# Two weight loads are moved behind later writes of x: the second expert tile's w1, and the quarters' first weights

## The chip, the cores and the metric

The kernel runs on one core of a Trainium2 chip. The metric is the device time of one execution in microseconds (us). A change under 0.3% (1.3 us) can hardly be told from no change here.

## The reference

Three layers run one after the other on 2 x 768 tokens of 512 numbers, in float32: decaying linear attention (8 heads), a feed-forward layer with a convolution along the sequence and a gate, and a mixture of 8 experts. Of the last two:

```
h = np.maximum(x @ w_in, 0.0)
...
return (h * gate @ w_out).astype(np.float32)
...
            h = np.maximum(x[b, s] @ w1[e], 0.0)
            out[b, s] = p[e] * (h @ w2[e])
```

The expert `e` of a token is the argmax of its eight logits, or the expert of the token before it where a local gate says so. So the tokens of one expert are known only when the second layer's output x is known.

## The kernel before

The second layer ends in `ffn_out`, which makes x in twelve tiles of 128 tokens: six of sequence 0 and six of sequence 1. Each tile is accumulated on TensorE (PE) into `x_ps` (lines 133 to 135), copied to SBUF by ScalarE (ACT, line 486), and written to the DRAM tensor `xs` by a DMA that SyncE (SP) issues (line 488). The copy of the last two tiles stays in SBUF as `xl`.

Around these tiles VectorE (DVE) makes the tables of the routing: `ei` (which expert each tile of the last layer uses) and `it` (which tokens it takes).

The last layer works in expert tiles of 128 tokens of one expert: 11 whole tiles, and two groups of four quarters of 32 tokens, each quarter with an expert of its own. A tile's tokens are brought from `xs` by an indirect DMA that GpSimd (POOL) issues (`gather`, line 724, into `xg`). The first two tiles, j = 0 and 1, gather from the first ten tiles of x alone; what they need of the last two comes on PE from `xl` by one-hot matrices (line 816). Every other gather reads all twelve tiles, the first of them that of the quarters' group 0 (`gather(NTILE)`), then that of tile 2.

Weights come over SP's queue, 512 KB for each DMA. `fetch(j, 0)` brings w1 of tile j in four DMAs into `r` (line 695), `fetch(j, 1)` w2; for j > 1 they are skipped when tile j - 2 had the same expert. `fetch_q(g, which, i)` brings an eighth of the weights of a group of quarters, one DMA for each of the four experts, into the buffers `qc` and `qs1l` in turn (line 705). A quarter's matmuls are `hq_ps` (line 889) and `yq_ps` (line 911).

The order of SP's queue is the order of the code. In the loop over `units` one pass adds two of the eight k-blocks to one tile of x, so passes 8, 12, 16 and 20 end tiles nine to twelve of x (t = 2 to 5 of sequence 1). Behind the loop `experts` begins with `fetch(1, 1)` and `fetch_q(0, 0, 1)`. Of SP's DMAs each waits until the one eight places ahead of it has landed (its lane, `DMAHW0` to `DMAHW7`), beside what its buffer needs.

Of the kernel before, what the change touches and what calls it, by code (L numbers as in the profile page):

```python
# [91 lines left out]
def tile_kernel(ctx, tc, cat, cst, qT, kT, kN, vN, w_in, conv_w, w_out, wg, w1, w2, out):  # L92
# [378 lines left out]
    def ffn_out(b, t, ms):  # L471

        ts = slice(t * P, (t + 1) * P)
        if ms[0] == 0:
            OUT[b, t] = psb.tile([P, DM], F32, tag="x2", name="x2_ps")
        ps = OUT[b, t]
        for m in ms:
            g = hg[b, m]
            mm3(ps, g[:, 0, ts], g[:, 1, ts], wo_hi[:, m, :], wo_lo[:, m, :], m == 0, m == 7)
        if ms[-1] == 7:  # L480
            if b == B - 1 and t >= NG - 2:
                xn = xpool[0].tile([P, DM], F32, name=f"xl{t}", bufs=1)
                LAST.append(xn)
            else:
                xn = rt.tile([P, DM], F32, name="xn", bufs=2)
            se.activation(out=xn, in_=OUT.pop((b, t)), func=AF.Copy)  # L486
            r = b * S + t * P
            sy.dma_start(out=xs[r:r + P, :], in_=xn)
# [183 lines left out]
    def home(tag):  # L672
        return big if tag[0] == "s" else ws if tag == "c4" else wx

    def expert_at(n):
        return sy.value_load(ei[0:1, 0, n:n + 1], min_val=0, max_val=E - 1)
# [6 lines left out]
    def fetch(j, which):  # L683

        src = (w1, w2)[which].rearrange("e p a n -> e p (a n)")
        kw = {}
        if j == 0:
            src = src[0]
        else:
            src = src[bass.ds(expert_at(j), 1)].rearrange("o p n -> (o p) n")  # L690
            if j > 1:
                kw = dict(cond=sy.value_load(ei[0:1, 1, j:j + 1], min_val=0, max_val=1), cond_hint=True)
        dst = raw(j % 2, which)
        for i in range(4):
            sy.dma_start(out=dst[:, i, :], in_=src[:, i * 1024:(i + 1) * 1024], **kw)

    def fetch_q(g, which, i):

        tag = QSLOT[nq[0] % 2]
        nq[0] += 1  # L700
        QW[g, which, i] = w = home(tag).tile([P, 4, 1024], F32, tag=tag, name="q" + tag)
        src = (w1, w2)[which].rearrange("e p a n -> e p (a n)")
        for u in range(4):
            one_e = src[bass.ds(expert_at(NTILE + 4 * g + u), 1)].rearrange("o p n -> (o p) n")
            sy.dma_start(out=w[:, u, :], in_=one_e[:, i * 1024:(i + 1) * 1024])

    def cut(j, which, i):

        tag = SLOT[ncut[0] % len(SLOT)]
        ncut[0] += 1  # L710
        w = home(tag).tile([P, 2, 2, 1024], F32R, tag=tag, name="w" + tag)
        for h in range(2):
            r = RAW[j % 2, which][:, 2 * i + h, :]
            se.activation(out=w[:, 0, h, :], in_=r, func=AF.Copy)  # L714
            ve.tensor_tensor(out=w[:, 1, h, :], in0=r, in1=w[:, 0, h, :].bitcast(F32), op=ALU.subtract)  # L715
        W[j, which, i] = w.rearrange("p s h n -> p s (h n)")
# [3 lines left out]
    def gather(j, n=NT):  # L720

        X[j] = xg = xpool[0].tile([P, DM], F32, name="xg")
        po.memset(xg, 0.0)
        return po.indirect_dma_start(out=xg, out_offset=None, in_=xs[0:n], in_offset=bass.IndirectOffsetOnAxis(ap=it[:, j:j + 1], axis=0),  # L724
                                     bounds_check=n - 1, oob_is_err=False)
# [43 lines left out]
    for n, (t, ms) in enumerate(units, 1):  # L769
        ffn_out(1, t, ms)  # L770
        for step in STEPS.get(n, ()):
            next(step, done)
        if n == 8:
            fetch(1, 0)
        if n in (10, 14):
            cut(0, 0, n // 14)
        if n == 13:
            fetch_q(0, 0, 0)
            for j in range(2):
                gather(j, NT - 2 * P)  # L780
    p2_stack.close()
    q_stack.close()
    lg_stack.close()
# [276 lines left out]
```

## Time and profile before

| | |
|---|---|
| time, median of 3 runs | 433.12 us (432.42 to 433.65) |
| profiled execution: its time, its span | 433.53 us, 431.8 us |
| PE busy | 406.7 us (94%) |
| DVE, ACT, POOL busy | 290.1, 259.4, 91.6 us |
| bytes by DMA, mean rate | 86.59 MB, 201 GB/s |
| granted TensorE clock, mean | 0.993 |

The span runs from the first to the last instruction of the one profiled execution; its time is 1.7 us longer. PE is busy nearly throughout, so the places where it is not are what a change of order can touch. The DMA engines carry 201 GB/s as a mean, but not evenly.

### The profile page before, as it was taken

The page shows a single profiled execution, that of the slowest core. Times are in us where ns is not written, and L with a number is a line of the kernel's source. Part 1 is how long each engine was busy: PE and PEld are TensorE (multiplying, and loading weights), DVE is VectorE, ACT ScalarE, POOL GpSimd, SP SyncE. Part 2 cuts the span into 40 slices and gives each one's busy share as a digit, 9 for nine tenths or more (in the row PEclk, how much of TensorE's full clock was granted, in tenths as well). Part 3 has the DMA queues.
Part 4 walks back from the last instruction along what each step waited for, and adds up shares of the span by engine and source line. Part 5 has one row for each costly group of instructions (what it writes and reads, how often), then busy time and mean ns, then how long its engine had stood idle before and what let it go on. Part 6 is the DMA issues. An engine that isn't in the chain of part 4 may idle for free.

```text
span 431.8 us, 7294 instructions
## 1 busy us (share of the span) xinstructions
PE 406.7 (94%) x2412; PEld 327.2 (76%) x2412; DVE 290.1 (67%) x518; ACT 259.4 (60%) x429; POOL 91.6 (21%) x92
## 2 busy tenths in 40 slices
PE   8898999997999999999999899999989999999991
PEld 7787897896898778989768676867738676776881
DVE  3798789798766350477899057968663796858650
ACT  2787677666755212566604166869555786958560
POOL 5256664213000000000000330205212132111210
PEclk9999999999999999999999999999999999999997
DMA  7989773320000101000296999999979999675001
GB/s 239 380 289 399 257 218 87 96 92 1 2 2 0 49 29 46 26 0 2 82 355 214 358 382 350 347 385 407 379 272 330 393 367 362 266 257 205 34 26 37
DMA packets 27324, 86.59 MB, mean 201 GB/s; under 512 B 3598, under 2 KB 4622, under 8 KB 27280
## 3 DMA queue, kind: packets, MB, share of 16 engines
q1 hardware_dynamic: 25200, 79.76, 50.6%
q0 software_dynamic: 2080, 6.29, 3.8%
q8 instruction: 21, 0.34, 0.3%
q14 instruction: 23, 0.19, 0.1%
HBM read 105.18 MB, written 6.55 MB: 259 GB/s over the span
## 4 chain that ended last, share of the span: by engine, by line
PE 35%; issue 26%; DMA 18%; DVE 14%; ACT 3%; POOL 2%; SPq 0%; POOLq 0%; DVEq 0%
DMA out_dram<-yo,it 15%; PE h_ps L133 5%; PE h_ps L135 4%; PE h_ps L134 4%; PE x_ps L133 4%; PE x_ps L134 3%; PE x_ps L135 3%; PE y L297 3%; PE s_ps L279 3%; DVE cc L350 2%; DMA kv<-in_kN_dram 2%; DVE na L149 2%; PE inc L287 2%; DVE na L150 1%; PE y L299 1%
## 5 line engine op out<-in xcount | busy, mean ns | idle before, releaser
L133 PE MATMUL h_ps<-xT,wih 128*128 128x384 f32 x128 | 46.5, 363 | 2.3 <-ACT wc L192 2.3
L350 DVE SCALAR_TENSOR_TENSOR cc<-h,cw,cc 128x768 f32<-128x768 f32 x32 | 35.1, 1097 | 16.8 <-ACT cc L347 16.8
L860 POOL DMA_INDIRECT out_dram<-yo,it x13 | 16.7, 1283 | 137.1 <-ACT yo L859 137.1
L724 POOL DMA_INDIRECT xg<-xs,it x13 | 18.8, 1442 | 125.5 <-DMA qc<-in_w_dram 118.6
L134 PE MATMUL h_ps<-xT,wih 128*128 128x384 f32 x128 | 43.1, 337 | 0.0
L135 PE MATMUL h_ps<-xT,wil 128*128 128x384 f32 x128 | 43.1, 336 | 0.0
L133 PE MATMUL x_ps<-woh,hg 128*128 128x512 f32 x96 | 38.5, 401 | 0.0
L134 PE MATMUL x_ps<-wol,hg 128*128 128x512 f32 x96 | 37.5, 391 | 0.0
L135 PE MATMUL x_ps<-woh,hg 128*128 128x512 f32 x96 | 37.5, 390 | 0.0
L715 DVE TENSOR_TENSOR ws0l<-r,ws0l 128x1024 fp32r<-128x1024 f32 x22 | 26.0, 1222 | 16.3 <-ACT ws0l L714 16.1
L297 PE MATMUL y<-at,vz 128*128 128x128 f32 x192 | 30.6, 281 | 1.7 <-DMA kv<-in_kN_dram 0.9
L715 DVE TENSOR_TENSOR ws0h<-r,ws0h 128x1024 fp32r<-128x1024 f32 x22 | 26.0, 1222 | 8.3 <-ACT ws0h L714 8.2
L715 DVE TENSOR_TENSOR wc<-r,wc 128x1024 fp32r<-128x1024 f32 x22 | 25.9, 1221 | 7.9 <-ACT wc L714 7.9
L714 ACT ACTIVATE ws0l<-r 128x1024 fp32r<-128x1024 f32 x22 | 22.1, 1052 | 13.6 <-PE y L135 13.6
L153 POOL TENSOR_TENSOR na<-na,raw 128x512 int32<-128x512 int32 (+1 forms) x17 | 21.9, 1290 | 38.2 <-DVE na L150 12.6
L715 DVE TENSOR_TENSOR ws1h<-r,ws1h 128x1024 fp32r<-128x1024 f32 x22 | 26.0, 1222 | 6.0 <-ACT ws1h L714 4.0
L279 PE MATMUL s_ps<-qz,kq 128*128 128x256 f32 x96 | 29.0, 384 | 1.0 <-DVE qz L248 1.0
L714 ACT ACTIVATE wc<-r 128x1024 fp32r<-128x1024 f32 x22 | 22.1, 1054 | 11.3 <-PE g L135 11.3
L297 PEld LDWEIGHTS y<-at,vz 128*128 128x128 f32 x192 | 25.3, 191 | 4.3 <-DVE xT L302 2.3
L133 PEld LDWEIGHTS h_ps<-xT,wih 128*128 128x128 f32 x128 | 24.1, 188 | 5.5 <-ACT wc L192 2.6
L281 DVE TENSOR_TENSOR at<-s_ps,ca 128x256 f32<-128x256 f32 x48 | 20.2, 420 | 11.6 <-PE s_ps L279 11.5
L486 ACT ACTIVATE xn<-x_ps 128x512 f32<-128x512 f32 x10 | 6.0, 599 | 32.8 <-PE x_ps L135 15.5
(231 smaller groups left out, 1041.5 us busy)
## 6 DMA issues: line engine op xcount, KB each, us to landing
r<-in_w_dram SPq DMA_DIRECT2D x88, 512.0 KB
qc<-in_w_dram SPq DMA_DIRECT2D x32, 512.0 KB
qs1l<-in_w_dram SPq DMA_DIRECT2D x32, 512.0 KB
raw<-in_w_in_dram SPq DMA_DIRECT2D x8, 512.0 KB
raw<-in_w_out_dram SPq DMA_DIRECT2D x8, 512.0 KB
kq<-in_qT_dram SPq DMA_DIRECT2D x7, 384.0 KB
kq<-in_kT_dram SPq DMA_DIRECT2D x7, 384.0 KB
kv<-in_vN_dram SPq DMA_DIRECT2D x7, 384.0 KB
```

The costliest lines, as they stand in the source:

```text
L133: te.matmul(ps, lhi, rhi, start=first, stop=False)
L134: te.matmul(ps, lhi, rlo, start=False, stop=False)
L135: te.matmul(ps, llo, rhi, start=False, stop=last)
L153: po.tensor_tensor(out=a, in0=a, in1=lo, op=ALU.add)
L279: te.matmul(ps, self.kq[:, 0, tok], self.qz[:, :, tok], start=True, stop=True)
L281: ve.tensor_tensor(out=self.at[c], in0=ps, in1=self.dm, op=ALU.mult)
L297: te.matmul(y, vz[:, c, j, :], at[:, j, :], start=(j == 0), stop=(c == 0 and j == 1))
L350: ve.scalar_tensor_tensor(out=cc, in0=h[:, i:i + S], scalar=cw[:, m, i:i + 1], in1=cc, op0=ALU.mult, op1=ALU.add)
L714: se.activation(out=w[:, 0, h, :], in_=r, func=AF.Copy)
L715: ve.tensor_tensor(out=w[:, 1, h, :], in0=r, in1=w[:, 0, h, :].bitcast(F32), op=ALU.subtract)
L724: return po.indirect_dma_start(out=xg, out_offset=None, in_=xs[0:n], in_offset=bass.IndirectOffsetOnAxis(ap=it[:, j:j + 1], axis=0), bound ...
L860: po.indirect_dma_start(out=out, out_offset=bass.IndirectOffsetOnAxis(ap=it[:, j:j + 1], axis=0), in_=yo, in_offset=None, bounds_check=NT ...
```

## The change

`fetch(1, 0)` moves from pass 8 (behind the write of tile nine of x) to pass 12 (behind that of tile ten). `fetch_q(0, 0, 0)` moves from pass 13 to pass 16 (behind the write of tile eleven). Nothing is added or removed.

```
         ffn_out(1, t, ms)
         for step in STEPS.get(n, ()):
             next(step, done)
-        if n == 8:
+        if n == 12:
             fetch(1, 0)
         if n in (10, 14):
             cut(0, 0, n // 14)
         if n == 13:
-            fetch_q(0, 0, 0)
             for j in range(2):
                 gather(j, NT - 2 * P)
+        if n == 16:
+            fetch_q(0, 0, 0)
```

SP's queue around the last four writes of x, before (`r_2127` is the buffer of `fetch(1, 0)`, `qc_2404` that of `fetch_q(0, 0, 0)`, `xn` and `xl` are tiles of x; of four like DMAs the first and the last stand here):

```order
L488 DMA xs<-xn 128x512 [waits DMAHW3_49,Activation_49]
L676 TENSOR_LOAD ei [waits DVE_49]
L695 DMA r_2127<-in_w_dram 128x1024 [waits DMAHW4_49]
...
L695 DMA r_2127<-in_w_dram 128x1024 [waits DMAHW7_49]
L488 DMA xs<-xn 128x512 [waits DMAHW0_49,Activation_49]
L705 DMA qc_2404<-in_w_dram 128x1024 [waits DMAHW1_49]
...
L705 DMA qc_2404<-in_w_dram 128x1024 [waits DMAHW4_49]
L488 DMA xs<-xl_2478 128x512 [waits DMAHW5_49,Activation_49]
L488 DMA xs<-xl_2506 128x512 [waits DMAHW6_49,Activation_49]
```

And the same place after the change (`qc_2440` is the buffer of `fetch_q(0, 0, 0)` there):

```order
L488 DMA xs<-xn 128x512 [waits DMAHW3_49,Activation_49]
L488 DMA xs<-xn 128x512 [waits DMAHW4_49,Activation_49]
L676 TENSOR_LOAD ei [waits DVE_49]
L695 DMA r_2127<-in_w_dram 128x1024 [waits DMAHW5_49]
...
L695 DMA r_2127<-in_w_dram 128x1024 [waits DMAHW0_49]
L488 DMA xs<-xl_2437 128x512 [waits DMAHW1_49,Activation_49]
L705 DMA qc_2440<-in_w_dram 128x1024 [waits DMAHW2_49]
...
L705 DMA qc_2440<-in_w_dram 128x1024 [waits DMAHW5_49]
L488 DMA xs<-xl_2506 128x512 [waits DMAHW6_49,Activation_49]
```

The write of tile ten now stands ahead of the four `r` loads, and the write of tile eleven ahead of the four `qc` loads; the write of tile twelve keeps its place and its lane.

POOL's gathers, a piece of the difference (the first row is the gather of tile 1, the two changed rows are that of the quarters' group 0, the last that of tile 2):

```order
 L724 DMA xg<-xs,it 128x512 [waits Pool_49]
 L723 MEMSET xg 128x512
-L724 DMA xg<-xs,it 128x512 [waits DMAHW6_49,DMAHW5_49,Pool_49]
+L724 DMA xg<-xs,it 128x512 [waits DMAHW6_49,DMAHW1_49,Pool_49]
 L723 MEMSET xg 128x512 [waits DMASW0_49,PE_49]
 L724 DMA xg<-xs,it 128x512 [waits Pool_49]
```

The order on POOL is the same; the group's gather waits, before and after, for the writes of tiles eleven and twelve, which are on lane 5 and lane 6 before, and on lane 1 and lane 6 after.

## Rows read from the trace of the kernel before

**Rows 1.** The page, the span in 40 slices of 10.8 us: DMA's busy tenths.

```profile
DMA  7989773320000101000296999999979999675001
```

**Rows 2.** Who PE waited for from 243 us on: total, times, longest.

```profile
PE tp L810 <- DMA xg<-xs,it: 2.0, 1, 2.0
PE yq_ps L911 <- DMA qs1l<-in_w_dram: 1.0, 1, 1.0
```

**Rows 3.** Timeline of PE, 242 to 246 us: start, us, instruction, idle before.

```profile
243.19 0.39 PE L135 MATMUL x_ps<-woh,hg 128*128 128x512 f32 x1
245.58 0.68 PE L810 MATMUL tp<-cs,xg 128*128 128x128 f32 x4 [2.00 <-DMA xg<-xs,it]
```

**Rows 4.** Timeline of PE, quarter matmuls at 282 and at 318 us.

```profile
282.51 1.90 PE L889 MATMUL hq_ps<-qs1l,xq 128*32 128x512 f32 x16
...
318.68 1.52 PE L911 MATMUL yq_ps<-qs1l,tq 128*32 128x512 f32 x4
321.24 2.99 PE L911 MATMUL yq_ps<-qs1l,tq 128*32 128x512 f32 x12 [1.04 <-DMA qs1l<-in_w_dram]
324.16 0.50 PE L133 MATMUL y<-ws0l,th 128*128 128x512 f32 x1
```

**Rows 5.** Timeline of SP's queue, 230 to 268 us: start, us over all of them.

```profile
230.05 1.95 SPq L695 DMA_DIRECT2D r<-in_w_dram  x4
232.11 0.55 SPq L488 DMA_DIRECT2D xs<-xn  x1
233.46 4.05 SPq L705 DMA_DIRECT2D qc<-in_w_dram  x4
238.79 5.78 SPq L488 DMA_DIRECT2D xs<-xl  x2
245.40 2.17 SPq L695 DMA_DIRECT2D r<-in_w_dram  x4
248.43 3.82 SPq L705 DMA_DIRECT2D qs1l<-in_w_dram  x4
253.77 8.95 SPq L695 DMA_DIRECT2D r<-in_w_dram  x8
263.97 3.69 SPq L705 DMA_DIRECT2D qc<-in_w_dram  x4
```

**Rows 6.** POOL's gathers: the first and third of five, and their landing.

```profile
240.02 1.21 POOL L724 DMA_INDIRECT xg<-xs,it  x1 [118.57 <-DMA qc<-in_w_dram]
247.52 1.00 POOL L724 DMA_INDIRECT xg<-xs,it  x1 [3.91 <-DMA xs<-xl]
...
DMA to landing us min/median/max: 4.0/7.3/8.1
```

**Rows 7.** The wait ahead of the first gather (ns min/median/max), and the last write's link in the chain.

```profile
L724 POOLq EVENT_SEMAPHORE  x5: 17/43/8201, 230.7 to 239.1; - x5
...
244.24 2.51 DMA xs<-xl
```

**Rows 8.** Windows: length, busy of PE, PEld, DVE, ACT, POOL, clock, DMA share, GB/s.

```profile
240.00:245.00 5.00, 3.58 (x16) 2.63 (x14) 0.00 (x0) 0.60 (x1) 3.30 (x4) 1.00 1.03 415
246.00:249.00 3.00, 3.00 (x29) 3.00 (x28) 0.00 (x0) 0.00 (x0) 1.48 (x2) 1.00 0.79 218
259.00:261.00 2.00, 2.00 (x10) 1.60 (x9) 1.43 (x2) 1.48 (x2) 0.00 (x0) 1.00 0.75 234
285.00:290.00 5.00, 5.00 (x28) 4.19 (x27) 1.80 (x2) 3.26 (x6) 0.00 (x0) 1.00 1.03 413
```

**Rows 9.** Timelines of DVE and PE: the table, and PE ahead of tile 1.

```profile
234.16 0.18 DVE L657 SCALAR_TENSOR_TENSOR it<-pl,pv 128x20 uint32<-128x20 f32 x1
...
256.82 0.60 PE L797 MATMUL tp<-cs,xg 128*128 128x128 f32 x4
258.16 0.50 PE L133 MATMUL g<-ws1h,xh 128*128 128x512 f32 x1 [0.74 <-ACT hr L848]
```

**Rows 10.** Who SP's queue waited for, 273 to 283 us.

```profile
SPq L705 <- PE hq_ps L889: 1.5, 1, 1.5
```

More of the change, by code (lines that the diff above doesn't have):

```diff
@@ L772, in tile_kernel @@
             next(step, done)
-        if n == 8:
+        if n == 12:
             fetch(1, 0)
@@ L777, in tile_kernel @@
         if n == 13:
-            fetch_q(0, 0, 0)
             for j in range(2):
                 gather(j, NT - 2 * P)
+        if n == 16:
+            fetch_q(0, 0, 0)
     p2_stack.close()
```

## The prediction

> **What bounds the kernel now.** I read the page first: the DMA engines are idle through the middle of the span, and from the slice that begins at 237 us on, a little past half way, they are at nine tenths or more for slice after slice [rows 1]. So the last layer, which begins near 243 us, is a stage in which PE works all the time while the DMA engines work all the time too. Next I asked the waits whom PE stands still for in that stage. There are two answers [rows 2]: 2.0 us for the gather `xg`, once, and a wait for `qs1l`, weights of a quarter.
>
> The timeline places them. The last matmul of x ends at 243.58 us (243.19 + 0.39) and the first transpose of expert tile 0 starts at 245.58 [rows 3]; that gap is what the moved loads stand next to. The other place is at 318 us. Sixteen quarter matmuls of one buffer take 1.90 us elsewhere; here four start at 318.68, the next twelve come in pieces, and the following instruction starts at 324.16 [rows 4]. That is 5.5 us for 1.9 us of work: PE stands for 3.6 us in all, though the waits name 1.0 of it. What it waits for is the last eighth of group 0's weights, four DMAs of 512 KB.
>
> How fast can the DMA engines go? At 285 us, with the queue full, they move 413 GB/s, and 415 at 240 us [rows 8]. So a 512 KB load costs 1.27 us of the stream, and a 256 KB write or gather 0.64. Between 246 and 249 us the rate falls to 218, which loses 3 x (1 - 218/413) = 1.4 us of stream; between 259 and 261 to 234, which loses 0.9 us [rows 8].
>
> **The change part by part.**
>
> *The write of tile ten.* Today it is issued at 232.11 us, behind four `r` loads issued from 230.05 [rows 5]. POOL waits 8.2 us for it, until 239.1, and the first gather follows at 240.02 [rows 6, 7]. The profile names a `qc` load as the last to come, but the gather needs only writes of `xs`, and four loads and a write (5.7 us of stream) behind the 2.5 us of a lone transfer from 230.05 end at 238.3, close to 239.1. With no load ahead, a write takes the 2.51 us of the last one [rows 7]: it lands at 234.6. The table `it` is there at 234.34 [rows 9], so it isn't late instead. The first gather then starts 0.9 us after the landing, as today: 235.5. Gathers take 4.0 to 8.1 us to land [rows 6], so it lands at 239.5 to 243.6, just ahead of PE's last matmul of x. The gap of 2.0 us closes: **-2.0 us at 243.6**. (Bounds: 0, if something else holds the gather; no more than 2.0, since PE has work up to 243.58.) The second gather follows two us later and is needed two us later.
>
> *The four `r` loads* move from 230.05 to the place where `qc` stands today, 1.35 us behind the write's issue: 233.46, so 3.4 us later [rows 5]. Their reader is `cut(1, 0, ..)`, which ACT runs behind the splits of x of tiles 0 and 1, so after 245 us; even behind both gathers they land by 242.3 us (233.46 + 2.5 + 4 x 1.27 + 2 x 0.64). Cost 0, covered by that work.
>
> *The four `qc` loads* move behind the write of tile eleven: 238.79 + 1.35 = 240.1 instead of 233.46, and their issue of 4.05 us [rows 5] ends at 244.2, where ACT delivers tile twelve. The write of tile twelve is therefore issued when it is today, and so are the loads at 245.40.
>
> *The write of tile twelve lands later.* Today the stream from the first `r` issue at 230.05 to that landing at 244.24 + 2.51 = 246.75 takes 16.7 us and holds eight loads, three writes and two gathers. After the change it begins at 233.46 with the same less one write (0.64): 233.46 + 16.7 - 0.64 = 249.5 us. The lower bound is 246.75, if the queue drains better than today; I take 249.2, **2.5 us later**. POOL's next gathers wait for exactly this write [rows 6]. Group 0's gather moves from 247.52 to 250.0 and lands, at the median of 7.3 us, at 257.3 (254.0 to 258.1). PE wants it for the transposes that start today at 256.82 [rows 9], and would now be there at 254.8. So PE waits there up to 3 us. Behind these transposes PE waits today 0.74 us for ACT before 258.16 [rows 9]; that slack goes too. With the gather at 257.3, the matmul of 258.16 starts between 257.9 and 258.2: of the 2.0 us, **0 to 0.3 us** are left there, 2.0 at best, and -0.5 at worst.
>
> *The stream behind it.* The loads issued from 245.40 on are now behind a write that lands 2.5 us later. But today the engines lose 1.4 us between 246 and 249, because the queue ran dry; a queue that is still full doesn't lose this. That leaves +1.1 us. The dip at 259 to 261 us, 0.9 us, comes while SP holds back loads until earlier ones have landed; some or all of it closes too if these land evenly. So the stream at 262 us is later by +0.2 to +1.1 us. Outer bounds: +2.5 if none of the dips closes, -0.9 if both close and the write is only 1.4 us late. I take **+0.2**, since both dips border on stretches at full rate.
>
> *Does this reach 318 us?* SP's issues from 263.97 on (four `qc`, then four `qs1l`, then `r`) follow one another with little slack: PE holds SP back once, 1.5 us near 282 [rows 10], and the DMA engines are full behind it [rows 8]. Hence the landing of the weights at 318 to 324 us moves with the stream and not with PE. PE arriving 2.0 us early would only stand there for 5.6 us instead of 3.6; PE arriving 0.5 late, for 3.1.
>
> **Sum.** Gap closed -2.0; group 0's gather +1.7 to +2.0; what is left of that, up to 2.0 us, swallowed by the 3.6 us stall; the stall's end moved by +0.2. Against the profiled execution, 433.53, this is 433.7; the median of the runs stands 0.4 us below it at 433.12, so the forecast is **433.3 us**, no change by a bound of 0.3% (1.3 us), which is about what this kernel's measurement can tell.
>
> **Rivals.**
>
> *Faster: the lead survives.* For this the weights at 318 us must land at least 1.3 us earlier. The mechanism: PE keeps its 2.0 us, frees the quarters' buffer earlier, SP issues from 263.97 on earlier, and the stream has closed its dips. Time: 433.1 - 2.0 = 431.1 at most, 431.8 at the bound. For it speaks that SP does wait for PE [rows 10]; against it that the stream begins 3.4 us later and can win back only 2.3. The lead itself hangs on how a gather fares beside a full SP queue. The five took 4.0 to 8.1 us [rows 6], a lone write 2.51 [rows 7], so they seem to queue behind SP's loads. [...] Chance 0.13.
>
> *Slower: the stream is the bound and starts late.* If the dips don't close, the whole delay of up to 2.5 us goes through to 318 us: 433.1 + 2.5 = 435.6, with half of them closed 434.4. It decides from a delay of 1.3 us on. For it: at 285 us and after, nothing in the stream has slack. Against it: the dips are there, and a stream that is late fills them. Chance 0.17.
>
> *The change doesn't do what it says.* The wait that ends at 239.1 could be that for the `qc` load, as named [rows 6]. After the change no `qc` load stands ahead of the gather, so the gap would close by this reading too. Only if the gather's own landing grew past 8 us, with four `r` loads just ahead of it, would the gap stay; then PE is where it is today and the stream still decides: 433.1 to 434.2. Chance 0.08, inside "no change" for the most part.
>
> **Chances and range.** No change (432 to 434.4, with the third rival in it) 0.70, faster 0.13, slower 0.17. The range for eight in ten reaches to half of each outer case: 431.9 to 434.8.
>
> **What would show it.** In the profile after: the first gather near 235.5; no idle time of PE ahead of L810; group 0's gather near 250 and a new wait of PE for `xg` at L797 near 255 to 257; the DMA engines without the dip at 246 to 249; the quarter matmuls at 318 us ending within 1 us of 324, with PE idle there for longer than 3.6 us if its lead survived that far. The prediction is wrong if those end more than 1.3 us earlier or later, or if PE's stall at 318 us turns out not to hang on the DMA stream.

## The result: 1% slower, and the profile after

The changed kernel takes 437.86 us (median of 8 runs, 436.06 to 439.11); the kernel before took 433.38 beside it. The ratio is 1.0086, 95% interval 1.0059 to 1.0112 (it is estimated from the runs and is not quite the quotient of the two medians, 1.0103): slower, where no change was forecast, and above the range. Ratios, intervals and means in this text leave out two executions in which the chip was in a slower state, one of e6 and one of the kernel before.

The profiled execution has a span of 437.3 us against 431.8, 5.5 us more. Not all of that is the change's. The tables' matmul `pl` (line 654), which runs ahead of the first place where a moved load can hold PE, starts at 232.48 us before and at 233.54 after: in this execution the granted clock was 0.50 from 106 to 109 us, in a stage that the change doesn't touch (the first 8 in the row of the clock below), and that start varies from 232.1 to 236.6 us over the kernels of this study. So I measure from the start of `pl`, and call such times "from pl". From pl to the end of the span it is 199.32 us before and 203.76 after, **4.44 us more**; the ratio of the times, 0.59% to 1.12% of 433.38, is 2.6 to 4.9 us.

The page, in slices of 10.9 us:

```profile
PEclk9999999998999999999999988999999999999998
DMA  7989673220000111000384997999988999775000
```

The clock row has a second fall, at 260 us, in the last layer; before, the mean clock was 0.993. Who PE waited for from 243 us on:

```profile
PE tp L798 <- DMA xg<-xs,it: 4.7, 1, 4.7
```

The wait of 2.0 us for the first gather [rows 2] is gone, and one of 4.7 us for group 0's gather has come. POOL's timeline shows both gathers (start, us):

```profile
236.28 1.21 POOL L724 DMA_INDIRECT xg<-xs,it  x1 [113.72 <-DVE pr L662]
...
253.34 1.53 POOL L724 DMA_INDIRECT xg<-xs,it  x1 [13.17 <-DMA xs<-xl]
```

The first is 3.7 us earlier than in [rows 6], and the profile names VectorE's work on the tables, no longer a DMA, as what it waited for. The second is 5.8 us later, 4.8 from pl. It waits for the write of tile twelve, whose flight stands in the chain of work that ended last:

```profile
245.31 7.26 DMA xs<-xl
```

7.26 us, against 2.51 [rows 7]. Group 0's gather itself then takes 7.2 us to land (the view of `xg` at 253 us):

```profile
DMA to landing us min/median/max: 7.2/7.2/7.2
```

SP's queue shows four `qc` loads issued right ahead of the write, the first of them 4.3 us ahead; in e9 below, with none there, the write takes 2.43 us.

```profile
234.49 1.95 SPq L695 DMA_DIRECT2D r<-in_w_dram  x4
239.85 0.34 SPq L488 DMA_DIRECT2D xs<-xl  x1
240.98 4.00 SPq L705 DMA_DIRECT2D qc<-in_w_dram  x4
245.31 0.33 SPq L488 DMA_DIRECT2D xs<-xl  x1
246.48 2.42 SPq L695 DMA_DIRECT2D r<-in_w_dram  x4
249.75 3.84 SPq L705 DMA_DIRECT2D qs1l<-in_w_dram  x4
255.12 9.73 SPq L695 DMA_DIRECT2D r<-in_w_dram  x8
269.31 3.69 SPq L705 DMA_DIRECT2D qc<-in_w_dram  x4
```

The rows from 246.48 to 255.12 are at most 1.4 us later than in [rows 5], 1.1 of it the late start. The last row is group 0's third eighth. It goes into the buffer `qc`, which held the first eighth, so PE must have read that before. It is 5.3 us later: between 264.85 (255.12 + 9.73) and 269.31 SP issues no DMA. The waits of SP name the reason, PE:

```profile
SPq L705 <- PE hq_ps L890: 5.8, 2, 3.6
```

PE's own timeline:

```profile
244.49 1.05 PE L811 MATMUL tp<-cs,xg 128*128 128x128 f32 x8
...
260.57 1.11 PE L798 MATMUL tp<-cs,xg 128*128 128x128 f32 x4 [4.75 <-DMA xg<-xs,it]
...
263.19 0.63 PE L134 MATMUL g<-ws1h,xh 128*128 128x512 f32 x1
...
267.33 1.93 PE L890 MATMUL hq_ps<-qc,xq 128*32 128x512 f32 x16
...
324.02 2.17 PE L912 MATMUL yq_ps<-qs1l,tq 128*32 128x512 f32 x4
326.38 1.04 PE L912 MATMUL yq_ps<-qs1l,tq 128*32 128x512 f32 x2 [0.18 <-DMA qs1l<-in_w_dram]
327.61 1.90 PE L912 MATMUL yq_ps<-qs1l,tq 128*32 128x512 f32 x10 [0.18 <-DMA qs1l<-in_w_dram]
```

The gap of [rows 3] is closed: tile 0 follows the last matmul of x without a wait. Then PE stands before 260.57, and the matmuls behind that take 0.63 us instead of 0.39. The stall over the last eighth of group 0's weights is still there, and still 5.5 us long (324.02 to 329.51, as from 318.68 to 324.23 [rows 4]), only later. The windows (columns as in [rows 8]) show the clock:

```profile
246.00:249.00 3.00, 3.00 (x29) 3.00 (x29) 0.00 (x0) 0.00 (x0) 0.00 (x0) 1.00 0.97 357
...
257.00:259.00 2.00, 0.00 (x0) 0.00 (x0) 0.00 (x0) 0.00 (x0) 1.67 (x3) 1.00 1.03 407
259.00:261.00 2.00, 0.43 (x2) 0.44 (x3) 0.00 (x0) 0.00 (x0) 0.00 (x0) 0.56 1.02 382
261.00:263.00 2.00, 2.00 (x8) 1.71 (x7) 0.00 (x0) 1.28 (x2) 0.00 (x0) 0.50 0.96 365
...
265.00:267.00 2.00, 2.00 (x11) 1.66 (x10) 0.66 (x1) 0.00 (x1) 0.00 (x0) 0.73 0.94 340
...
269.00:271.00 2.00, 2.00 (x21) 0.49 (x13) 1.94 (x2) 2.00 (x4) 0.00 (x0) 1.00 0.36 49
```

PE idles from about 255.8 us; the granted clock falls from 1.00 to 0.50 between 259 and 259.5 us, and is back at 1.00 near 266. And the DMA engines, which the prediction took to be full from here on, move 49 GB/s at 269 to 271: SP has given them nothing.

### The profile page after: what moved, and what is told of

The parts are those of the page before. It is cut to its first block, busy times and chain, and to the rows that moved or that the text cites. A ratio compares the mean times of both kernels' runs of the same rounds, so it can differ in the third digit from the quotient of the medians.

```text
span 437.3 us, 7294 instructions
## 1 busy us (share of the span) xinstructions
PE 410.9 (94%) x2412; PEld 331.0 (76%) x2412; DVE 290.0 (66%) x518; ACT 259.7 (59%) x429; POOL 92.8 (21%) x92
## 4 chain that ended last, share of the span: by engine, by line
PE 31%; issue 26%; DMA 18%; DVE 16%; ACT 5%; POOL 2%; SPq 1%; POOLq 0%; DVEq 0%; ACTq 0%
DMA out_dram<-yo,it 14%; PE h_ps L133 4%; PE x_ps L133 4%; DVE cc L350 3%; PE x_ps L134 3%; PE x_ps L135 3%; PE h_ps L134 3%; PE y L297 3%; PE h_ps L135 3%; PE s_ps L279 2%; DMA xs<-xl 2%; DVE na L149 2%; DVE cc L354 1%; DMA kq<-in_qT_dram 1%; PE inc L287 1%
## 5 line engine op out<-in xcount | busy, mean ns | idle before, releaser
L133 PE MATMUL h_ps<-xT,wih 128*128 128x384 f32 x128 | 47.2, 368 | 2.3 <-ACT wc L192 2.3
L724 POOL DMA_INDIRECT xg<-xs,it x13 | 20.0, 1541 | 129.9 <-DVE pr L662 113.7
L861 POOL DMA_INDIRECT out_dram<-yo,it x13 | 16.7, 1282 | 135.8 <-ACT yo L860 135.8
L134 PE MATMUL h_ps<-xT,wih 128*128 128x384 f32 x128 | 43.7, 341 | 0.0
```

Source lines behind the costliest of these rows:

```text
L133: te.matmul(ps, lhi, rhi, start=first, stop=False)
L134: te.matmul(ps, lhi, rlo, start=False, stop=False)
L861: po.indirect_dma_start(out=out, out_offset=bass.IndirectOffsetOnAxis(ap=it[:, j:j + 1], axis=0), in_=yo, in_offset=None, bounds_check=NT ...
```

## Experiments

All kernels are compared in one table, worked from their timelines. "PE frees" is the end of the sixteen matmuls `hq_ps<-qc,xq` of group 0's first eighth; "SP issues" the issue of the third eighth into the same buffer `qc`; both as they stand in the trace. The last three columns are differences to before, measured from pl: that issue, the end of the stall over the last eighth (the last `yq_ps<-qs1l` of group 0), and the end of the span.

| kernel | pl | PE frees | SP issues | issue | stall over | end |
|---|---|---|---|---|---|---|
| before | 232.48 | 263.90 | 263.97 | 0 | 0 | 0 |
| after | 233.54 | 269.26 | 269.31 | +4.28 | +4.22 | +4.44 |
| e3: r moved alone | 232.09 | 267.20 | 267.26 | +3.68 | +3.94 | +4.49 |
| e4: qc moved alone | 233.40 | 266.83 | 266.89 | +2.00 | +2.04 | +1.88 |
| e1: group 0 later | 236.63 | 272.61 | 272.67 | +4.55 | +5.13 | +5.65 |
| e2: long filler | 234.46 | 272.05 | 272.12 | +6.17 | +5.42 | +4.92 |
| e5: short filler | 235.09 | 268.31 | 268.37 | +1.79 | +1.20 | +1.19 |
| e6: PE late ahead | 232.95 | 269.17 | 269.23 | +4.79 | +3.91 | +3.83 |
| e7: PE late behind | 234.92 | 265.83 | 265.90 | -0.51 | +0.55 | +1.26 |
| e8: write held | 233.20 | 263.32 | 264.05 | -0.64 | -1.30 | -0.92 |
| e9: qc behind the last write | 232.69 | 261.95 | 268.54 | +4.36 | +3.45 | +2.79 |
| e10: held and swapped | 233.38 | 263.06 | 263.97 | -0.90 | -2.48 | -2.30 |

Each row is one execution; the times beside the runs below are medians of 6 or 12, and their ratios are to the kernel before, run beside them.

**e3, the r loads alone** (against the changed kernel):

```
         if n == 13:
+            fetch_q(0, 0, 0)
...
-        if n == 16:
-            fetch_q(0, 0, 0)
```

> The first half of the change alone: w1 of tile 1 behind the write of tile ten, the quarters' first weights where they were, now right behind. Gather theory: eight loads run without a gap ahead of the write of tile twelve, it lands near 249, the group's gather at 256 to 257, PE waits for it 1.5 to 2 us, about what the closed gap gave: 433 to 434.5 us. Stream theory: the first loads are as late as in the changed kernel, 436.5 to 438 us.

437.03 us, ratio 1.0048 (1.0022 to 1.0073): slower.

```profile
PE tp L797 <- DMA xg<-xs,it: 3.9, 1, 3.9
```

The link of the last write in its chain:

```profile
243.85 6.49 DMA xs<-xl
```

**e4, the qc loads alone:**

```
-        if n == 12:
+        if n == 8:
             fetch(1, 0)
```

> The second half alone: the quarters' first weights behind the write of tile eleven, w1 of tile 1 where it was. Gather theory: the gap of 2.0 us at the first gather stays, the write of tile twelve stands behind four late loads and lands near 249, so PE, which comes 2 us later than in the changed kernel, waits 0.5 to 2 us for the group's gather: 434 to 436 us. Stream theory: the stream starts in time, within 1 us of before.

436.95 us, ratio 1.0044 (1.0017 to 1.007): slower.

```profile
PE tp L798 <- DMA xg<-xs,it: 2.4, 1, 2.4
PE tp L811 <- DMA xg<-xs,it: 0.9, 1, 0.9
```

Each part alone makes group 0's gather late: it starts 19.0 us from pl in e3 and 19.1 in e4, against 15.0 before. Each puts loads closer ahead of the write of tile twelve: the first of the last four is issued 8.1 us ahead of it in e3 and 4.3 in e4, against 10.8 before. In e4 the first gap shrinks too, from 2.0 to 0.9 us. By the one profile of each the parts overlap in what they cost (+4.49 and +1.88 us, together +4.44); by the times they add up (0.48% and 0.44%, together 0.86%), so whether they overlap is not shown. No half of the change is worth keeping.

**e1, group 0's quarters one turn later**, so that other work of PE stands where it waited:

```
-    QT = [2, 3, 8, 8, 9, 13, 17] + [18, 21, 26, 26, 27, 31, 36]
+    QT = [3, 3, 8, 8, 9, 13, 17] + [18, 21, 26, 26, 27, 31, 36]
```

> The changed kernel, but PE takes up group 0's tokens one hook later (QT begins with 3 instead of 2), so that a product of tile 1 stands ahead of the transposes which wait for the group's gather. Gather theory (the loss is PE waiting 4.7 us for this gather, and what follows from that wait): the wait shrinks under 1 us, the clock stays at its upper level, 431.5 to 433.5 us. Stream theory (the loss is that the weight loads start late and the DMA stream stays late): nothing changes, 437 to 438.5 us.

440.21 us, ratio 1.0118 (1.0073 to 1.0162).

```profile
PE hq_ps L890 <- ACT xq L882: 4.0, 1, 4.0
...
PE tp L798 <- DMA xg<-xs,it: 0.4, 1, 0.4
```

A miss: the wait for the gather was down to 0.4 us, but ACT's copy `xq` now stood behind its cuts of other weights (`ws0l` and `ws1h`), PE waited 4.0 us for it, and the clock fell (0.57 from 267 to 270 us). It doesn't tell the theories apart. All it adds is that PE was late again and the end with it.

**e2 and e5, filler on PE.** Eleven, then five matmuls of no use stand ahead of the transposes of group 0's tokens, to keep PE busy while it would wait (each is two instructions in the trace). This adds work:

```
+        if g == 0:
+            w = psb.tile([P, 512], F32, tag="b", name="fill")
+            for _ in range(5):
+                te.matmul(w, ident, cs[:, 0:512], start=True, stop=True)
         ps = turn(X.pop(NTILE + g), 0)
```

> The changed kernel with 11 extra matmuls (whose result nobody reads, some 4.9 us) ahead of the transposes that wait for group 0's gather: PE works while it would have waited. If the fall of the TensorE clock after the wait is a part of the loss, the clock stays at its upper level and the time falls by 2 to 2.8 us, to 435 to 436. If the loss is the wait alone, or the late stream alone, it stays at 437.5 to 438.5 us.

> The changed kernel with 5 extra matmuls (10 instructions of 0.44 us, 4.4 us, nobody reads them) ahead of the transposes that wait for group 0's gather, about as long as PE waits there, so that the gather sets the end of the stretch as before. Clock theory (a part of the loss is that TensorE runs at its lower level after the wait): no stretch at the lower level near 260 us, the first quarter matmuls come 2 to 2.5 us earlier against the tables' matmul than in the changed kernel, and the time falls by the same to about 435.5. If the wait alone makes the loss: as the changed kernel, 437.9, or up to 0.7 above it.

Eleven: 441.18 us, ratio 1.0151 (1.0111 to 1.0191). They took 9.6 us, twice what I meant, so PE came later than with the wait, 6.2 us late at the quarters, and this run says nothing on the clock's price. Five: 435.65 us, ratio 1.0027 (1.0003 to 1.0051), 0.6% below the changed kernel's ratio although five matmuls of work were added. The windows and PE's timeline of e5:

```profile
259.00:261.00 2.00, 2.00 (x6) 0.86 (x5) 0.00 (x0) 0.00 (x0) 1.25 (x2) 1.00 1.02 396
261.00:263.00 2.00, 1.50 (x8) 0.81 (x7) 0.00 (x0) 0.16 (x1) 0.00 (x0) 1.00 0.91 349
```

```profile
262.15 0.66 PE L798 MATMUL tp<-cs,xg 128*128 128x128 f32 x4 [0.50 <-DMA xg<-xs,it]
...
266.38 1.93 PE L894 MATMUL hq_ps<-qc,xq 128*32 128x512 f32 x16
```

The gather comes no earlier (the transposes stand 27.06 us from pl, after 27.03), but the clock stays at 1.00, and from the transposes to the first quarter matmul it takes 4.23 us instead of 6.76 (267.33 - 260.57). So the fall of the clock costs **2.5 us** there, and the end comes 3.25 us earlier from pl.

**e6 and e7, PE late without the change.** The kernel before, with four such matmuls (3.6 us) ahead of group 0's transposes, or the same four behind its first matmuls `hq_ps`, ahead of `turn(hq, ..)`, near 289 us. These add work too. If the stall at 318 us swallows PE's lateness, as the prediction had it, both do as little; if PE sets when the third eighth is fetched, only the first does harm.

```
+        if g == 0:
+            w = psb.tile([P, 512], F32, tag="b", name="fill")
+            for _ in range(4):
+                te.matmul(w, ident, cs[:, 0:512], start=True, stop=True)
```

> The kernel before, loads where they were, with 4 extra matmuls (3.5 us) ahead of the transposes of group 0's tokens, that is ahead of the first quarter matmuls. Pacing theory (SP can't issue the next quarter weights until PE has read the first, so PE's lateness there goes into the DMA stream and to the end): the first quarter matmuls come 2.8 us later, and the time grows by 2.5 to 3 us, to 436.5 to 437. Absorption theory (the prediction's: the stall of 3.6 us at 318 us hangs on the stream alone and swallows it): 0 to 0.7 us slower.

> The kernel before with the same 4 extra matmuls (3.5 us), now behind group 0's four hidden products, ahead of the transposes at 287 us, where no weight buffer waits to be freed soon. Both theories: the stall at 318 us shrinks from 3.6 us to near 0 and the time stays within 0.7 us of before. If it grows by 2.5 us or more, the place doesn't matter and PE's work alone sets the time.

e6: 436.29 us, ratio 1.0022 (0.9993 to 1.0051). e7: 433.83 us, ratio 0.9993 (0.9964 to 1.0022). Neither differs clearly from the kernel before. From each other they do: both were run on the same chip in the same session, and the mean of e6, 436.06 us, is 1.8 us above that of e7, 434.24 (95% interval 0.5 to 3.1). The traces show why. SP's queue and PE in e6:

```profile
269.23 4.47 SPq L705 DMA_DIRECT2D qc<-in_w_dram  x4
```

```profile
267.25 1.92 PE L893 MATMUL hq_ps<-qc,xq 128*32 128x512 f32 x16
...
322.20 1.92 PE L915 MATMUL yq_ps<-qc,tq 128*32 128x512 f32 x16
...
326.71 1.90 PE L915 MATMUL yq_ps<-qs1l,tq 128*32 128x512 f32 x10 [0.19 <-DMA qs1l<-in_w_dram]
```

And in e7:

```profile
265.90 3.70 SPq L705 DMA_DIRECT2D qc<-in_w_dram  x4
```

```profile
263.91 1.92 PE L889 MATMUL hq_ps<-qc,xq 128*32 128x512 f32 x16
...
322.27 1.92 PE L915 MATMUL yq_ps<-qc,tq 128*32 128x512 f32 x16
...
325.32 1.90 PE L915 MATMUL yq_ps<-qs1l,tq 128*32 128x512 f32 x10 [0.28 <-DMA qs1l<-in_w_dram]
```

In both PE comes late to the stall, by 4.80 us in e6 (322.20 - 232.95, against 316.93 - 232.48) and by 2.90 in e7. In e7 the stall swallows all but 0.55 of it. In e6 3.91 are left, where a stall with 3.6 us to give would have left 1.2. (In e6's profile PE was also 0.8 us longer in the gap ahead of tile 0 and the clock fell there, 0.56 from 249 to 252 us, so its lateness is more than the filler.) The difference is whether PE is late ahead of or behind the matmuls that free `qc`.

**e8, a cure for the gap by the other end.** In the kernel before, the write of tile nine is held until the `r` loads have been issued, so that SP need not wait for it ahead of them:

```
-    OUT = {}
+    OUT, HELD = {}, []
...
-            sy.dma_start(out=xs[r:r + P, :], in_=xn)
+            write = lambda: sy.dma_start(out=xs[r:r + P, :], in_=xn)
+            if (b, t) == (1, 2):
+                HELD.append(write)
+            else:
+                write()
...
         if n == 8:
             fetch(1, 0)
+            HELD.pop()()
```

> Another way to close the gap: the kernel before, with the write of tile nine issued behind w1 of tile 1 instead of ahead of it, so that these loads start when the tables are ready, some 3 us earlier, while the DMA engines are idle; nothing is loaded later than before. Gather theory: the write of tile ten lands some 3 us earlier, the gap at the first gather closes, the write of tile twelve and group 0's gather stay where they are, PE comes up to 1.7 us earlier to the first quarter matmuls; 0.3 to 1.5 us faster than before, 431.9 to 433.1 against 433.4. If a closed gap must be paid for later in any order of the loads: no faster than before.

433.95 us, ratio 0.9985 (0.9956 to 1.0015): the same. In its profile the gap shrinks from 2.0 to 0.7 us and PE frees `qc` 1.3 us earlier from pl, but SP is not there yet: it issues 0.7 us behind PE's end. Here the stream is the later of the two.

**e9, the q loads behind the last write** (against the changed kernel):

```
-        if n == 16:
+        if n == 20:
             fetch_q(0, 0, 0)
```

> The changed kernel, with the quarters' first weights behind the write of tile twelve instead of that of tile eleven; nothing else differs. Times from the tables' matmul pl on. Theory A (the write of tile twelve is late because four loads stand right ahead of it; group 0's gather, PE's wait, the clock and the pacing of the next quarter loads follow from that): the write lands within 3 us of its issue instead of 7.3, the gather of group 0 starts within 17.5 us of pl, PE waits under 2 us for it instead of 4.7, the clock keeps its upper level, the first quarter matmul is at 28 to 30.5 us, and the end is within 1.3 us of before: 433 to 435 us. Rival B (the loads as such come too late, wherever the writes stand): the gather is early, but the weights that now start 5 us later push the stream, and the end is 2 to 4 us later than before with PE on time at the first quarter matmul: 436 to 438 us.

438.13 us, ratio 1.0116 (1.0077 to 1.0155): as slow as the change itself, so rival B. (The profiled execution was the fastest of the six.) Its chain, POOL, PE and SP:

```profile
244.45 2.43 DMA xs<-xl
```

```profile
247.65 1.00 POOL L724 DMA_INDIRECT xg<-xs,it  x1 [8.33 <-DMA xs<-xl]
```

```profile
254.83 0.60 PE L798 MATMUL tp<-cs,xg 128*128 128x128 f32 x4
...
263.48 1.05 PE L890 MATMUL hq_ps<-qs1l,xq 128*32 128x512 f32 x2 [1.52 <-DMA qs1l<-in_w_dram]
```

```profile
258.71 8.98 SPq L695 DMA_DIRECT2D r<-in_w_dram  x8
268.54 3.70 SPq L705 DMA_DIRECT2D qc<-in_w_dram  x4
```

With no load right ahead of it the write flies 2.43 us, group 0's gather starts 15.0 us from pl as before, PE doesn't wait for it, and the clock stays at 1.00 from 240 to 273 us: this half of theory A holds. The end does not. The first two eighths, fetched some 5 us later than in the changed kernel, keep PE waiting for `qs1l` at 263.48, and SP's issue of `r` loads ends at 267.69 (258.71 + 8.98), so that the third eighth is issued 6.6 us after PE has freed its buffer. PE frees `qc` 2.2 us earlier from pl than before, and the end still comes 2.8 us later, since the stream is late.

**e10, e8 with the second eighth fetched ahead of w2 of tile 1:**

```
-        fetch(1, 1)
         fetch_q(0, 0, 1)
+        fetch(1, 1)
```

> The kernel before, with the write of tile nine held until behind the r loads (as in the run with the held write), and with the quarters' second eighth fetched ahead of w2 of tile 1. Theory A (the end follows PE's lateness at the first quarter matmuls, and the order of two loads that both land before they are read does not matter): as with the held write alone, 0 to 1 us faster than before: 433.2 to 434.2 us. Rival B (the stream's order counts, since the weights of the stall at 318 us stand behind these): the stall there shrinks by the 1 to 2 us that the quarters' loads are issued earlier: 431.5 to 433 us; or w2 of tile 1 comes late and PE waits for it: over 435 us.

434.22 us, ratio 1.0006 (0.9977 to 1.0035): the same. Its one profile ends 2.3 us earlier from pl, but the runs don't bear that out, so no version here beats the kernel before.

## Why the prediction was wrong

**The step that failed** is the one that made the forecast "no change": "the landing of the weights at 318 to 324 us moves with the stream and not with PE", with what was built on it, that PE's lead or lag is swallowed by the 3.6 us stall. In the kernel before, SP's issue of the third eighth at 263.97 [rows 5] stands 0.07 us behind the end of PE's matmuls on the buffer that it refills, 261.98 + 1.92 = 263.90:

```profile
261.98 1.92 PE L889 MATMUL hq_ps<-qc,xq 128*32 128x512 f32 x16
```

The waits of SP from 263 to 273 us in the kernel before name PE too:

```profile
SPq L705 <- PE hq_ps L889: 0.4, 1, 0.4
```

The prediction put that issue under "the stream" and looked for PE's hold on SP only 18 us later [rows 10]. Its rival "faster" did name the link (PE frees the buffer earlier, SP issues from 263.97 on earlier), but only for a lead of PE, and the sum left it out. In the table SP issues 0.05 to 0.07 us behind PE wherever PE is the later one (before, after, e1 to e7), and 0.7 to 6.6 us behind it where the stream is (e8 to e10). The end follows this issue within about 1.8 us in every row, whichever of the two set it; e7, where PE is late only behind it, loses 1.3 us of 3.6 added. In the changed kernel SP waited 3.6 us for PE there.

**Terms that were mis-sized** made PE so late. Gap closed: forecast -2.0, it closed as described, with the first gather off the write's path. Write of tile twelve: forecast 2.5 us later, measured 4.8 from pl (252.57 - 233.54, against 246.75 - 232.48). The prediction gave the stretch from the first `r` issue to that landing 16.7 us as before, less one write: 16.06. It took 18.08 (234.49 to 252.57). What the engines moved in it, before (230.05 to 246.75) and after:

```profile
DMA packets 1786, 5.58 MB, mean 334 GB/s; under 512 B 224, under 2 KB 224, under 8 KB 1786
DMA packets 1913, 6.34 MB, mean 351 GB/s; under 512 B 233, under 2 KB 233, under 8 KB 1912
```

They were not slower. They moved 0.76 MB more, although one write of 0.26 MB less belongs to the stretch. So about 1.0 MB of the loads that SP issued behind the write was carried before the write had landed. At 413 GB/s that is 2.5 us, enough for the 2.0 us by which the stretch is longer, and the prediction's sum had nothing pass the write. Counting four loads of 1.27 us and a write of 2.51 from the write's issue on gives 7.6 us, near the 7.26 of its flight, but that is luck. The same count would hold for e3, where the first of the four is issued 8.1 us ahead of the write instead of 4.3 and the flight is 6.49, and for the kernel before, where it is issued 10.8 us ahead and the flight is 2.51. Group 0's gather: 7.2 us to land, as forecast from the median of 7.3, so it came 2.3 us later than forecast with its write. PE's wait: up to 3 us forecast, 4.7 measured. **A term that was missing** is the clock: 2.5 us, by e5. Together: from pl, PE is 2.69 us late at the transposes (27.03 against 24.34) and 4.29 at the first quarter matmul; the 1.60 between are the clock's 2.5 less the slack of 0.74 [rows 9] that is gone, and 0.2 unaccounted for.

**What held.** The stream's own delay: SP's eight `r` loads begin 0.3 us and end 1.1 us later from pl (255.12 and 264.85, against 253.77 and 262.72), inside the forecast +0.2 to +1.1; the dip at 246 to 249 us did close, 357 GB/s instead of 218. Had the failed step been true, PE 4.3 us late at a stall with 3.6 us to give would have left 0.7 us, less than the stream's own 1.1, and the time would have stayed inside the range. The rival "slower" named a late stream, which is not what happened in the changed kernel, but is what e9 shows. The third rival, a first gather that takes over 8 us, did not come: it landed in 7.4. The rival "faster" hung on how a gather fares beside SP's full queue: group 0's took 7.2 us to land there, within the 4.0 to 8.1 us of [rows 6].

**What stays open.** Times and profiles agree in sign for the change, e3, e4 and e9. But the ends in the table are of one execution each, and for e3, e6, e7, e9 and e10 they lie 0.3 to 1.6 us outside the interval of the times. For e6 the profile says +3.8 us, the ratio's interval reaches 1, and against e7 the runs say 0.5 to 3.1: that lateness ahead of the freed buffer costs more than lateness behind it is shown by both, its price only roughly. No run gave the third eighth a buffer of its own, which would test the link directly.

## What to carry to other kernels

When a queue's issue stands as close behind the end of the instructions that free its buffer as SP's did here (0.05 to 0.07 us), take the engine as what sets that issue, however small the wait that a view sums up (0.4 us here). PE's delay went through to what that load feeds: in the changed kernel +4.28 us at the issue, +4.22 at the end of the stall. A lead counted only until the queue became the later one: in e8 PE was 1.3 us earlier from pl and the issue 0.64. Look for writes that others wait for with loads close ahead of them on their queue: here such a write took 7.26 us to land instead of 2.51, and about 1 MB of the loads issued behind it was carried before it landed. And price a new wait of PE with the slow matmuls that may follow it: here 2.5 us behind a wait of 4.75.

## What the runs showed of the hardware

**Loads issued behind a write were carried before it landed.** With four 512 KB loads right ahead, a 256 KB write took 7.26 us to land, and about 1.0 MB of later loads, by the sums of bytes above, was carried before that; with none right ahead (e9) it took 2.43.

**The price of a fall of the clock.** An idle stretch of PE of 4.75 us cost a further 2.5 us: when PE worked again, at 260.57, the granted clock was 0.50, and it was back at 1.00 near 266; the 2.5 us are the difference to e5, where it stayed at 1.00. In e4 the fall came after a wait of only 2.4 us:

```profile
257.00:259.00 2.00, 0.00 (x0) 0.00 (x0) 0.23 (x1) 0.91 (x2) 1.11 (x1) 1.00 1.04 405
259.00:261.00 2.00, 1.77 (x6) 1.58 (x7) 0.00 (x0) 0.61 (x2) 0.00 (x0) 0.50 1.01 392
```

The 2.0 us gap of the kernel before [rows 3] was followed by a clock of 1.00 [rows 8]. The length of a wait alone doesn't tell: near 105 us, ahead of the stage in question, PE waits 2.31 us both before and after the change; before, the clock is 1.00 there in each microsecond from 104 to 109, and after, it is 0.50 from 106 to 109. In the changed kernel's trace the windows between 0.50 and 1.00 near 260 us (0.56, 0.73) are means over a change: in narrower windows the clock is 1.00 up to 259 us, 0.50 throughout from 259.5 to 266, and 1.00 from 266.25 to 300.
